# Attention and soft-MoE on one core: larger input loads, far masks on VectorE, and single-bank PSUM tiles in the tail

## The chip, the core and the metric

The kernel runs on one core of one Trainium2 chip. The metric is device time in microseconds (us). A core has TensorE (PE, matmuls, its weight loads shown apart as PEld), VectorE (DVE), ScalarE (ACT), GpSimd (POOL), SyncE (SP) and 16 DMA engines. All operands of matmuls lie in SBUF; results go to PSUM[...].

## The reference, cut to what matters

```python
# q, k, v: (4 batches, 8 heads, 768 positions, 64), all float32
scores = (q @ k.transpose(0, 1, 3, 2)) / 8.0
causal = rel >= 0                                   # rel = row position - column position
stream_keep = causal & (is_sink | (rel < 64))       # is_sink: the first 4 columns
mask = where(is_retrieval[head], causal, stream_keep)
a = softmax(where(mask, scores, -1e9))              # over the columns
x = (a @ v).transpose(0, 2, 1, 3).reshape(3072, 512)

logits = x @ phi                                    # phi: (512, 32); 8 experts, 4 slots each
d = softmax(logits, axis=0)                         # over the tokens
slot_input = (d.T @ x).reshape(8, 4, 512)
slot_out[e] = relu(slot_input[e] @ w1[e]) @ w2[e]   # w1: (512, 1024), w2: (1024, 512) per expert
out = softmax(logits, axis=1) @ slot_out            # (3072, 512) float32
```

Three of the eight heads are "retrieval" heads (full causal mask), the others keep a window of 64 and the first four columns. Which head is which is an input that is read on the chip.

## The kernel before

The order of all work is written out by hand (a manual schedule): each engine runs its instructions in the order in which the program names them, and the framework adds the semaphore waits. The work has three stages.

**Attention** goes over 16 pairs of heads, `n` from 0 to 15 (pairs 0 to 3 are batch 0, and so on). `load_qk` (L104) and `load_v` (L111) bring the pair's q, k and v from memory; DMAs issued on POOL turn float32 into bf16 on the way. `transposes` (L135) turns q or k on PE, `evac` (L143) copies the result out of PSUM, q on DVE, k on ACT. `scores` (L159) makes one of six chunks of the transposed scores and their exponentials on ACT (L171); `mask` (L173) multiplies chunks by the mask on DVE; `vfar` (L153) multiplies the far blocks of v by `fmask`; `pvmm` (L185) multiplies by v, `norm` (L195) divides by the row sums. The loop at L318 is pipelined: iteration `n` makes the scores of pair `n`, the PV products of pair `n-1`, and the transposes of q and k of pair `n+1`; q's come after the second chunk of scores in PE's order, k's after the fourth.

The loads run ahead. Iteration `n` issues k, q and v of pair `n+3` (L319 to L322), and one or two half weight matrices (`w_load`, L119: 26 halves of `w1` and of the first five `w2`). The raw tiles of q and k have three buffers, v has five tiles (`vbs`, L100). Two things hold an issue back on POOL: a buffer still in use, and the framework's eight DMA semaphores: a DMA waits for the eighth one before it. All these DMAs go through one queue.

`fmask` (per head and far block, whether a key counts) is filled at the start by ACT, two copies for each of eight heads (L301 to L303).

**Routing** is woven into the loop: per batch, `x_transpose`, `logits_mm`, `logits_exp`, `exp_tokens` and `dispatch_mm` make the logits, their exponentials and the unnormalized slot inputs; `slot_sum` adds the latter over the batches. The last batch does this after the loop (L398 to L419). There all six token blocks go to one PSUM tile, which ACT and DVE copy by halves (L254, L255).

**The tail.** The last three `w2` matrices have no place of their own: `w2_5` takes the masks' place, `w2_6` and `w2_7` that of the probabilities, so their loads (L389 to L408) wait for the end of the loop. From L427 on: slot inputs (`sip`, `siT`), first layer into the two-bank tiles `hp` (L439), ReLU by ACT on one half and DVE on the other (L443, L444), transposes of the hidden layer (L450), row sums for the output (`rp`, L462), and the second layer (`second`, L467), where four experts stand side by side on 32 output partitions each. `sp` is copied to `slot_out` by halves (L476, L477). Then 24 blocks of 128 output rows (L479 to L492): a matmul into half of a two-bank tile `op`, even rows read by DVE, odd rows by ACT, and a DMA on SP after 1, 1, 2 and then each 4 rows.

Of the kernel before, what the change touches and what calls it, by code (L numbers as in the profile page):

```python
# [10 lines left out]
F32 = mybir.dt.float32  # L11
BF16 = mybir.dt.bfloat16
I32 = mybir.dt.int32
ALU = mybir.AluOpType
ACT = mybir.ActivationFunctionType
# [3 lines left out]
NP = 16  # L19
# [19 lines left out]
def kernel(  # L39
# [13 lines left out]
    nc = tc.nc  # L53
    P = 128
    B, H, S, D = q.shape
    n_sink, window = int(n_sink), int(window)
    ES = moe_phi.shape[1]
    NE, DM, F = moe_w1.shape
    SPE = ES // NE
    scale = 1.0 / (D ** 0.5)  # L60
    ent = ctx.enter_context
# [3 lines left out]
    raw = ent(tc.tile_pool(name="raw", bufs=3))  # L65
    qkT = ent(tc.tile_pool(name="qkT", bufs=2))
# [3 lines left out]
    xp = ent(tc.tile_pool(name="xp", bufs=2))  # L70
    scp = ent(tc.tile_pool(name="scp", bufs=2, space=PSUM))
# [3 lines left out]
    def single(shape, dt, name, tag=None):  # L75
        return singles.tile(shape, dt, name=name, tag=tag or name)
# [3 lines left out]
    ident = single([P, P], BF16, "ident")  # L80
# [7 lines left out]
    slot_bf = single([P, 2, DM], BF16, "slot_bf")  # L88
# [11 lines left out]
    vbs = [single([P, 2, 6, 66], BF16, f"vb{i}") for i in range(5)]  # L100
# [3 lines left out]
    def load_qk(n, which):  # L104
        b, h = n // 4, 2 * (n % 4)
        src, d = (q, qraw) if which == "q" else (k, kraw)
        t = raw.tile([P, 2, 384], BF16, tag="r" + which, name="r" + which)
        nc.gpsimd.dma_start(t, src[b, h:h + 2].rearrange("h (p s) d -> p h (s d)", s=6))  # L108
        d[n] = t

    def load_v(n):  # L111
        b, h = n // 4, 2 * (n % 4)
        a = v[b, h:h + 2]
        nc.gpsimd.dma_start(vbs[n % 5].rearrange("p h j d -> p (h j) d")[:, :, :D],  # L114
                            a.rearrange("h (j p) d -> p (h j) d", p=P))
# [3 lines left out]
    def w_load(count):  # L119
        for _ in range(count):  # L120
            i = wi[0]
            wi[0] += 1
            if i >= 4 * NE - 6:
                return
            e, half = (i % (2 * NE)) // 2, i % 2
            if i < 2 * NE:
                nc.gpsimd.dma_start(  # L127
                    w1s[e][:, 2 * half:2 * half + 2, :],
                    moe_w1[e].rearrange("(di do) f -> di do f", do=4)[:, 2 * half:2 * half + 2, :])
            else:  # L130
                nc.gpsimd.dma_start(
                    w2s[e][:, 4 * half:4 * half + 4, :],
                    moe_w2[e].rearrange("(fi fo) d -> fi fo d", fo=8)[:, 4 * half:4 * half + 4, :])
# [19 lines left out]
    def vfar(n):  # L153
        h = 2 * (n % 4)
        t = vfp.tile([P, 2, 4, 66], BF16, tag="vf", name="vf")
        nc.vector.tensor_mul(t, vbs[n % 5][:, :, :4, :], fmask[:, h:h + 2])
        vf[n] = t
# [27 lines left out]
    def pvmm(n, i):  # L185
        if i % 3 == 0:
            pv[n] = pvp.tile([P, 3, 2, 65], F32, tag="pv", name="pv")
        for hh in range(2):
            for j in range(i + 1):
                vv = vbs[n % 5] if i - j <= 1 else vf[n]  # L190
                o = BLK[j, i]
                nc.tensor.matmul(pv[n][:, i % 3, hh, :], pT[n][:, hh, o:o + 128], vv[:, hh, j, :D + 1],  # L192
                                 start=(j == 0), stop=(j == i))
# [43 lines left out]
    def dispatch_mm(b, i0=0, i1=6):  # L237
        if i0 == 0:
            sps[b] = pvp.tile([P, DM], F32, tag="pv", name="slp")
        for i in range(i0, i1):  # L240
            g = i % 4
            nc.tensor.matmul(sps[b][32 * g:32 * g + 32, :], elgs[b][:, i, :], xb[b][:, i, :],
                             start=(i < 4), stop=(i + 4 >= 6))

    def slot_sum(b):
        sp = sps[b]
        if b == 0:
            nc.vector.tensor_copy(slot_acc, sp)
        elif b == B - 2:
            nc.vector.tensor_add(slot_bf[:, 0], slot_acc, sp)  # L250
        elif b < B - 1:
            nc.vector.tensor_add(slot_acc, slot_acc, sp)
        else:
            nc.scalar.copy(slot_bf[:, 1, :256], sp[:, :256])  # L254
            nc.vector.tensor_copy(slot_bf[:, 1, 256:], sp[:, 256:])  # L255


    load_qk(0, "k")
    load_qk(0, "q")
# [6 lines left out]
    load_qk(1, "k")  # L266
    load_qk(1, "q")
    load_v(1)
    w_load(1)
    load_qk(2, "k")  # L270
    load_qk(2, "q")
    load_v(2)
# [27 lines left out]
    V.memset(vbs[0][:, :, :, D:], 1.0)  # L300
    for h in range(H):  # L301
        nc.scalar.copy(fmask[:, h], r1[:, h:h + 1].rearrange("p (o d) -> p o d", o=1).to_broadcast([P, 4, 66]))
        nc.scalar.copy(fmask[:, h, 0], r0[:, h:h + 1].to_broadcast([P, 66]))  # L303
    for t in vbs[1:]:
        V.memset(t[:, :, :, D:], 1.0)

# [11 lines left out]
    for n in range(NP):  # L318
        if n + 3 < NP:  # L319
            load_qk(n + 3, "k")  # L320
            load_qk(n + 3, "q")
            load_v(n + 3)  # L322
        w_load(2 if n % 3 == 2 else 1)
# [54 lines left out]
        if n < 3:  # L378
            for h in (2 * n + 2, 2 * n + 3):
                head_mask(h)  # L380
        elif n == 3:
            setup_late()


    w_load(4 * NE)
# [3 lines left out]
    def w2_late(e):  # L389
        for half in range(2):  # L390
            nc.gpsimd.dma_start(w2s[e][:, 4 * half:4 * half + 4], w2v[e][:, 4 * half:4 * half + 4])  # L391

    w2_late(5)
    w2s[6] = ptp.tile([P, 8, DM], BF16, tag="pT", name="w2_6")
    w2_late(6)
# [12 lines left out]
    w2_late(7)  # L408
# [10 lines left out]
    slot_sum(bl)  # L419
# [7 lines left out]
    sip = trp.tile([P, 4, ES], F32, tag="tr", name="sip")  # L427
    sv = [slot_bf[:, x].rearrange("p (di do) -> p do di", do=4) for x in range(2)]
    for do in range(4):
        for x in range(2):  # L430
            nc.tensor.matmul(sip[:, do], sv[x][:, do], sum4, start=(x == 0), stop=(x == 1))
    V.tensor_copy(siT, sip)
    hs = []
    for e4 in range(2):
        hp = scp.tile([P, 2, 512], F32, tag="sc", name="hp")
        for c in range(2):
            for do in range(4):
                for g in range(4):
                    nc.tensor.matmul(hp[32 * g:32 * g + 32, c], siT[:, do],  # L439
                                     w1s[4 * e4 + g][:, do, c * 512:(c + 1) * 512],  # L440
                                     start=(do == 0), stop=(do == 3))
        t = xp.tile([P, 2, 512], BF16, tag="xb", name="hs")
        nc.scalar.activation(t[:, 0], hp[:, 0], ACT.Relu, scale=emask[:, e4:e4 + 1])  # L443
        V.tensor_scalar(t[:, 1], hp[:, 1], emask[:, e4:e4 + 1], 0.0, op0=ALU.mult, op1=ALU.max)  # L444
        hs.append(t.rearrange("p c f -> p (c f)").rearrange("p (fi fo) -> p fo fi", fo=8))
    hT = []
    for e4 in range(2):
        tp = trp.tile([P, 8, P], BF16, tag="tr", name="tph")
        for fo in range(8):
            nc.tensor.transpose(tp[:, fo, :], hs[e4][:, fo, :], ident)  # L450
        t = qkT.tile([P, 8, P], BF16, tag="hT", name="hT")
        if e4 == 0:
            V.tensor_copy(t, tp)
        else:
            nc.scalar.copy(t, tp)
        hT.append(t)
    rp = trp.tile([P, 24], F32, tag="tr", name="rp")
# [6 lines left out]

    sp = pvp.tile([P, DM], F32, tag="pv", name="sp")

    def second(e4, gs):  # L467
        for fo in range(8):
            for g in gs:
                nc.tensor.matmul(sp[32 * g:32 * g + 32, :], hT[e4][:, fo, 32 * g:32 * g + 32],  # L470
                                 w2s[4 * e4 + g][:, fo, :],
                                 start=(e4 == 0 and fo == 0), stop=(e4 == 1 and fo == 7))

    for e4, gs in ((0, (0, 1, 2, 3)), (1, (0, 1)), (1, (2,)), (1, (3,))):
        second(e4, gs)
    V.tensor_copy(slot_out[:, :256], sp[:, :256])  # L476
    nc.scalar.copy(slot_out[:, 256:], sp[:, 256:])  # L477
# [3 lines left out]
    for t, rows in enumerate((1, 1, 2, 4, 4, 4, 4, 4)):  # L481
        ot = single([P, rows, DM], F32, f"ot{t}", tag=f"w1_{t}")
        for y in range(0, rows, 2):
            op = scp.tile([P, 2, DM], F32, tag="sc", name="op")
            for x in range(min(2, rows)):
                nc.tensor.matmul(op[:, x], er[r], slot_out, start=True, stop=True)  # L486
                if r % 2:
                    nc.scalar.activation(ot[:, y + x], op[:, x], ACT.Copy, scale=rrow[:, r:r + 1])  # L488
                else:
                    V.tensor_scalar(ot[:, y + x], op[:, x], rrow[:, r:r + 1], None, op0=ALU.mult)  # L490
                r += 1
        nc.sync.dma_start(ov[:, r - rows:r, :], ot)  # L492
# [35 lines left out]
```

The softmax here doesn't subtract the row's maximum and nothing guards it: scores larger than these inputs give would overflow.

## Time and profile before

| | us |
|---|---|
| median of 6 runs (lowest, highest) | 170.03 (169.53, 170.54) |
| the profiled execution | 169.53 |
| its span on the core | 167.7 |
| busy PE, PEld | 121.1, 71.7 |
| busy DVE, ACT, POOL | 102.0, 113.6, 58.5 |

Busy times are unions of an engine's instructions, of a span of 167.7 us. POOL's busy time is nearly all the making of DMA descriptors (0.7 us for a q or k, 1.02 for a v, 0.56 for half a weight). The memory traffic is 52.50 MB read and 6.29 MB written. In the page, a line such as "L171 ACT" names line 171 of the kernel; the 40 digits of a row are tenths of busy time in 40 equal slices of the span. In the chain of waits each row has a start, a duration and an instruction, and the row above is what it waited for. In the timeline, a bracket tells how long the engine had been idle and what ended that.

### The profile page before, as it was taken

The numbers are of one execution on the slowest core, as the hardware profiler recorded it, in microseconds if no ns is written. First come the engines' busy times: TensorE is split into PE (matmuls) and PEld (weight loads), VectorE is DVE, ScalarE is ACT, GpSimd is POOL, SyncE is SP. The second block draws the span as 40 slices with busy tenths as digits, with TensorE's granted clock in tenths as the row PEclk, the third lists the DMA queues.
The fourth block names the chain that finished last, engine by engine and source line by source line (L and its number), as shares of the span: only waits on it lengthen the run. The fifth ranks groups of instructions, "written<-read, shape, count | busy, mean of one in ns | idle before, by whom it ended". The sixth has DMA issues, their size and how long they took to land. (4 is left out here: it accounts for less than half of the span.)

```text
span 167.7 us, 4099 instructions
## 1 busy us (share of the span) xinstructions
PE 121.1 (72%) x1752; PEld 71.7 (43%) x1752; DVE 102.0 (61%) x226; ACT 113.6 (68%) x162; POOL 58.5 (35%) x89
## 2 busy tenths in 40 slices
PE   0455987977969977969979787988597965555430
PEld 0332555654546555636556555556235621111100
DVE  2846489999839879836898756887305004334410
ACT  3699899999888999977999978892312102334330
POOL 7994555563554454462542615006100000000000
PEclk9999999999999999996999996999969996555555
DMA  3999999999999999999999999999999941566665
GB/s 48 145 180 190 201 193 194 192 212 191 204 198 193 210 193 195 201 200 204 198 192 196 210 193 211 212 213 217 211 214 212 216 86 44 206 250 250 250 279 221
DMA packets 39985, 32.80 MB, mean 196 GB/s; under 512 B 26656, under 2 KB 34848, under 8 KB 39328
## 3 DMA queue, kind: packets, MB, share of 16 engines
q0 software_dynamic: 38672, 26.25, 105.3%
q1 hardware_dynamic: 1296, 6.30, 9.2%
q8 instruction: 13, 0.21, 0.5%
q14 instruction: 4, 0.03, 0.0%
HBM read 52.50 MB, written 6.29 MB: 351 GB/s over the span
## 5 line engine op out<-in xcount | busy, mean ns | idle before, releaser
L171 ACT ACTIVATE pT<-sc 128x1024 bf16<-128x1024 f32 (+1 forms) x96 | 83.5, 928 | 8.4 <-PE sc L166 7.6
L166 PE MATMUL sc<-Tq,Tk 64*128 64x256 bf16 (+3 forms) x320 | 37.4, 301 | 16.7 <-ACT Tk L150 9.0
L192 PEld LDWEIGHTS <-pT 128*128 128x128 bf16 x672 | 25.0, 99 | 11.3 <-issue 8.3
L183 DVE TENSOR_TENSOR pT<-pT,msk 128x1024 bf16<-128x1024 bf16 (+1 forms) x48 | 29.3, 640 | 0.1
L192 PE MATMUL pv<-vb,pT 128*128 128x65 bf16 x352 | 27.5, 197 | 0.0
L192 PE MATMUL pv<-vf,pT 128*128 128x65 bf16 x320 | 25.2, 197 | 0.0
L114 POOL DMA_DIRECT2D vb<-in_v_dram x16 | 16.5, 1032 | 22.2 <-DVE pT L183 5.2
L166 PEld LDWEIGHTS <-Tk 64*128 64x128 bf16 x320 | 12.2, 96 | 27.4 <-ACT Tk L150 11.8
L486 PE MATMUL op<-slot_out,expT 128*128 128x512 bf16 x24 | 12.3, 606 | 10.6 <-DVE ot L490 9.7
L201 DVE TENSOR_TENSOR xb<-pv,rs 128x384 bf16<-128x384 f32 x32 | 17.8, 557 | 1.1
L147 DVE COPY Tq<-tpq 128x768 bf16<-128x768 bf16 x16 | 15.3, 957 | 4.9 <-PE tpq L140 4.9
L488 ACT ACTIVATE ot<-op,rrow 128x512 f32<-128x512 f32 x12 | 8.2, 687 | 14.5 <-PE op L486 14.5
L200 DVE RECIPROCAL rs<-pv 128x6 f32<-128x6 f32 x32 | 6.2, 194 | 18.3 <-PE pv L192 18.2
L490 DVE TENSOR_SCALAR ot<-op,rrow 128x512 f32<-128x512 f32 x12 | 9.0, 751 | 12.8 <-PE op L486 12.8
L150 ACT COPY Tk<-tpk 128x768 bf16<-128x768 bf16 x16 | 13.0, 814 | 3.6 <-PE tpk L140 3.6
L108 POOL DMA_DIRECT2D rk<-in_k_dram x16 | 11.5, 718 | 7.2 <-PE sc L166 3.2
L140 PE MATMUL tpk<-ident,rk 128*64 128x128 bf16 x192 | 9.1, 234 | 5.3 <-DMA rk<-in_k_dram 4.7
L108 POOL DMA_DIRECT2D rq<-in_q_dram x16 | 11.5, 716 | 2.8 <-DMA vb<-in_v_dram 2.6
L127 POOL DMA_DIRECT2D w<-in_moe_w_dram x16 | 9.0, 565 | 8.3 <-DMA w<-in_moe_w_dram 7.4
L140 PE MATMUL tpq<-ident,rq 128*64 128x128 bf16 x192 | 10.0, 251 | 2.4 <-DMA rq<-in_q_dram 2.4
L486 PEld LDWEIGHTS <-expT 128*128 128x128 bf16 x24 | 3.8, 157 | 17.7 <-issue 17.7
L140 PEld LDWEIGHTS <-rk 128*64 128x64 bf16 x192 | 6.5, 116 | 8.9 <-DMA rk<-in_k_dram 4.7
(70 smaller groups left out, 118.2 us busy)
## 6 DMA issues: line engine op xcount, KB each, us to landing
w<-in_moe_w_dram POOLq DMA_DIRECT2D x32, 512.0 KB, 12.3
out_dram<-ot SPq DMA_DIRECT2D x5, 1024.0 KB, 3.8
rk<-in_k_dram POOLq DMA_DIRECT2D x16, 192.0 KB, 11.3
rq<-in_q_dram POOLq DMA_DIRECT2D x16, 192.0 KB, 11.5
vb<-in_v_dram POOLq DMA_DIRECT2D x16, 192.0 KB, 10.8
out_dram<-ot SPq DMA_DIRECT2D x2, 256.0 KB, 2.2
out_dram<-ot SPq DMA_DIRECT2D x1, 512.0 KB, 2.6
phi<-in_moe_phi_dram POOLq DMA_DIRECT2D x1, 32.0 KB, 11.1
```

Source lines behind the costliest of these rows:

```text
L108: nc.gpsimd.dma_start(t, src[b, h:h + 2].rearrange("h (p s) d -> p h (s d)", s=6))
L114: nc.gpsimd.dma_start(vbs[n % 5].rearrange("p h j d -> p (h j) d")[:, :, :D], a.rearrange("h (j p) d -> p (h j) d", p=P))
L127: nc.gpsimd.dma_start(w1s[e][:, 2 * half:2 * half + 2, :], moe_w1[e].rearrange("(di do) f -> di do f", do=4)[:, 2 * half:2 * half + 2, :])
L140: nc.tensor.transpose(tp[64 * hh:64 * hh + 64, s, :], src[:, hh, 64 * s:64 * s + 64], ident)
L147: nc.vector.tensor_copy(o, i)
L150: nc.scalar.copy(o, i)
L166: nc.tensor.matmul(sc[:, hh, at:at + 128 * cnt], kT[n][po:po + 64, j * 128:(j + 1) * 128], qT[n][po:po + 64, i0 * 128:(i0 + cnt) * 128], s ...
L171: nc.scalar.activation(pT[n][:, :, o:o + ln], sc[:, :, :ln], ACT.Exp, scale=scale)
L183: nc.vector.tensor_mul(x, x, m)
L192: nc.tensor.matmul(pv[n][:, i % 3, hh, :], pT[n][:, hh, o:o + 128], vv[:, hh, j, :D + 1], start=(j == 0), stop=(j == i))
L201: nc.vector.tensor_mul(xb[b][:, 3 * half:3 * half + 3, h * D:(h + 2) * D].rearrange("p i (h d) -> p i h d", h=2), pv[n][:, :, :, :64], rs. ...
L486: nc.tensor.matmul(op[:, x], er[r], slot_out, start=True, stop=True)
```

## The change

- q and k are loaded for four heads (two pairs) in one DMA, from pair 2 on; pairs 0 and 1 keep loads of two heads. v is loaded for four heads from the start. In odd iterations `n`, the loads of pairs `n+3` and `n+4` are issued. Raw tiles have two buffers of twice the size, v has three tiles of twice the size.
- A weight matrix is one DMA, and the pace is written as a total: `w_load(upto)`. Only `w2_7` keeps two halves.
- The far masks are made by DVE, two copies for two heads at a time: the first pair's at the start, the others' in iterations 0 to 2.
- In the last batch the six token blocks go to two PSUM tiles of three blocks each; both are copied by DVE, and `sip` sums three terms instead of two.
- From `sip` on, PSUM tiles are one bank for one reader (`bank`): `hp` per half, the transposes of the hidden layer four at a time with one copy each on DVE and ACT, `sp` as two tiles of 256 columns (so `second` has twice the matmuls, each of 256 columns), and `op` one row per tile, from six tiles in turn.
- The order of the tail on PE changes: transposes of the first four experts, their second layer, transposes of the others, second layer of experts 4 and 5, `rp`, then experts 6 and 7.

```diff
-    raw = ent(tc.tile_pool(name="raw", bufs=3))
+    raw = ent(tc.tile_pool(name="raw", bufs=2))
...
-    vbs = [single([P, 2, 6, 66], BF16, f"vb{i}") for i in range(5)]
+    vbs = [single([P, 4, 6, 66], BF16, f"vb{i}") for i in range(3)]
...
+    def load_qk(pairs, which):
+        b, h, c = pairs[0] // 4, 2 * (pairs[0] % 4), 2 * len(pairs)
...
+        t = raw.tile([P, c, 384], BF16, tag="r" + which, name="r" + which)
+        nc.gpsimd.dma_start(t, src[b, h:h + c].rearrange("h (p s) d -> p h (s d)", s=6))
+        for x, n in enumerate(pairs):
+            d[n] = t[:, 2 * x:2 * x + 2]
...
+    def w_load(upto):
+        while wi[0] < min(upto, 2 * NE - 3):
+            e = wi[0] % NE
+            if wi[0] < NE:
+                nc.gpsimd.dma_start(w1s[e], moe_w1[e].rearrange("(di do) f -> di do f", do=4))
+            else:
+                nc.gpsimd.dma_start(w2s[e], moe_w2[e].rearrange("(fi fo) d -> fi fo d", fo=8))
+            wi[0] += 1
...
+    load_qk([0], "k")
+    load_qk([0], "q")
...
     load_v(0)
-    load_qk(1, "k")
-    load_qk(1, "q")
-    load_v(1)
-    w_load(1)
-    load_qk(2, "k")
-    load_qk(2, "q")
-    load_v(2)
+    load_qk([1], "k")
+    load_qk([1], "q")
     w_load(1)
...
-    for h in range(H):
-        nc.scalar.copy(fmask[:, h], r1[:, h:h + 1].rearrange("p (o d) -> p o d", o=1).to_broadcast([P, 4, 66]))
-        nc.scalar.copy(fmask[:, h, 0], r0[:, h:h + 1].to_broadcast([P, 66]))
-    for t in vbs[1:]:
+    def far_mask(n):
+        h = 2 * n
+        V.tensor_copy(fmask[:, h:h + 2, 1:], r1[:, h:h + 2].rearrange("p (h a d) -> p h a d", a=1, d=1).to_broadcast([P, 2, 3, 66]))
+        V.tensor_copy(fmask[:, h:h + 2, 0], r0[:, h:h + 2].rearrange("p (h d) -> p h d", d=1).to_broadcast([P, 2, 66]))
+
+    for t in vbs:
         V.memset(t[:, :, :, D:], 1.0)
+    far_mask(0)
+    load_qk([2, 3], "k")
+    load_qk([2, 3], "q")
+    load_v(1)
+    w_load(2)
...
     for n in range(NP):
-        if n + 3 < NP:
-            load_qk(n + 3, "k")
-            load_qk(n + 3, "q")
-            load_v(n + 3)
-        w_load(2 if n % 3 == 2 else 1)
+        if n % 2 == 1 and n + 4 < NP:
+            for which in ("k", "q"):
+                load_qk([n + 3, n + 4], which)
+            load_v((n + 3) // 2)
+        w_load(2 + (5 * (n + 1) + 1) // 7)
...
         if n < 3:
+            far_mask(n + 1)
             for h in (2 * n + 2, 2 * n + 3):
                 head_mask(h)
...
-    slot_sum(bl)
+    V.tensor_copy(slot_bf[1][:96], sps[bl, 0][:96])
+    V.tensor_copy(slot_bf[2][:96], sps[bl, 3][:96])
...
+    def bank(t, shape=(P, 512), dt=F32):
+        pool, tag = ((scp, "sc"), (trp, "tr"), (pvp, "pv"))[t]
+        return pool.tile(list(shape), dt, tag=tag, name="bank")
...
-        hp = scp.tile([P, 2, 512], F32, tag="sc", name="hp")
+        t = xp.tile([P, 2, 512], BF16, tag="xb", name="hs")
         for c in range(2):
+            hp = bank(0 if e4 == 0 else 2)
...
+    def turn(e4):
+        t = qkT.tile([P, 8, P], BF16, tag="T" + "qk"[e4], name="hT")
+        for x in range(2):
+            tp = bank(1, (P, 4, P), BF16)
+            for fo in range(4):
+                nc.tensor.transpose(tp[:, fo, :], hs[e4][:, 4 * x + fo, :], ident)
+            if x:
+                nc.scalar.copy(t[:, 4:], tp)
+            else:
+                V.tensor_copy(t[:, :4], tp)
+        hT[e4] = t
+
+    sp = [bank(0, (P, 256)) for x in range(2)]
+
+    def second(e4, gs):
+        for fo in range(8):
+            for x in range(2):
+                for g in gs:
+                    nc.tensor.matmul(sp[x][32 * g:32 * g + 32, :], hT[e4][:, fo, 32 * g:32 * g + 32],
+                                     w2s[4 * e4 + g][:, fo, 256 * x:256 * x + 256],
+                                     start=(e4 == 0 and fo == 0), stop=(e4 == 1 and fo == 7))
+
+    turn(0)
+    second(0, (0, 1, 2, 3))
+    turn(1)
+    second(1, (0, 1))
+    rp = bank(1, (P, 24))
...
+    second(1, (2,))
+    second(1, (3,))
+    V.tensor_copy(slot_out[:, :256], sp[0])
+    nc.scalar.copy(slot_out[:, 256:], sp[1])
...
-        for y in range(0, rows, 2):
-            op = scp.tile([P, 2, DM], F32, tag="sc", name="op")
-            for x in range(min(2, rows)):
-                nc.tensor.matmul(op[:, x], er[r], slot_out, start=True, stop=True)
...
+        for y in range(rows):
+            op = bank((1, 2, 0)[r % 3])
+            nc.tensor.matmul(op, er[r], slot_out, start=True, stop=True)
+            if r % 2:
+                nc.scalar.activation(ot[:, y], op, ACT.Copy, scale=rrow[:, r:r + 1])
+            else:
+                V.tensor_scalar(ot[:, y], op, rrow[:, r:r + 1], None, op0=ALU.mult)
+            r += 1
```

## The prediction

> **What bounds the kernel now.** I read the slices of the page first, then the chain of waits, then the DMA issues, then the timelines of GpSimd (POOL) and TensorE (PE).
>
> ```profile
> DMA  3999999999999999999999999999999941566665
> GB/s 48 145 180 190 201 193 194 192 212 191 204 198 193 210 193 195 201 200 204 198 192 196 210 193 211 212 213 217 211 214 212 216 86 44 206 250 250 250 279 221
> ```
>
> A slice is 4.19 us. The DMA engines are full from slice 1 to slice 31 (134 us): the kernel reads 52.5 MB in one stream. After it they are half busy.
>
> ```profile
> 118.42 19.38 DMA w<-in_moe_w_dram
> 137.79 0.04 issue
> 137.84 1.04 PE sp L470 x4
> 138.87 0.02 issue
> 138.90 0.43 DVE slot_out L476
> 139.33 0.02 issue
> 139.35 0.38 ACT slot_out L477
> ...
> 144.48 1.02 PE op L486 x2
> 145.51 0.03 issue
> 145.53 0.76 DVE ot L490
> 146.29 0.04 issue
> ```
>
> The chain: the last weight lands at 137.8, `sp` is done at 138.87, and then 28.8 us of output follow. There a pair of rows takes 1.85 us, since matmuls and both readers take turns on one two-bank `op` tile. Before 137.8 there is slack: PE waited 1.43 us for that weight (L470), so `sp` could have ended at 138.87 - 1.6 = 137.27.
>
> In the attention loop ScalarE (ACT) sets the pace: 5.7 us a pair, some 8 in pairs 5, 9, 13. What can break this pace is the arrival of q and k. Two answers about pair 14's q, the issue and the time to landing, and PE's use of it:
>
> ```profile
> 81.80 0.71 POOL L108 DMA_DIRECT2D rq<-in_q_dram  x1
> ```
> ```profile
> DMA to landing us min/median/max: 12.0/12.0/12.0
> ```
> ```profile
> 94.72 0.53 PE L140 MATMUL tpq<-ident,rq 128*64 128x128 bf16 x12
> ```
>
> It lands at 93.8 and is transposed at 94.7: under 1 us to spare. Landings follow the order of issue. In a full queue a k or q of two heads adds 0.99 us, a v 1.27, half a weight 2.45 (the last six land at 125.5, 128.0, 130.5, 132.9, 135.3, 137.8).
>
> **What the Trainium skill says.** "DMA: Bandwidth & Descriptors", section Bandwidth: larger DMAs are better, 341 GB/s at 1 MB, 425 at 16 MB, and 435 is the ceiling. Here half a weight is 1.05 MB of f32 in 2.45 us, 428 GB/s: queued behind others it is already there, so size can bring 1.6% of the weights' time. "PSUM — Partial Sum Buffer", section PSUM bank collisions: two engines may not use one bank at once. The trace agrees: ACT's `slot_out` starts 0.02 us after VectorE's (DVE) has ended. "TensorE: Matmul & The Clock Gate", section LDWEIGHTS: time goes with the columns, by its formula an estimated 27 ns for 32; the trace has 43 ns (L439, 0.17 for four). Same page, Part 1: an idle PE drops to half clock; granted here was 0.50 from 140 us on.
>
> **The change, part by part.**
>
> *Loads of four heads, whole weights.* The same bytes and rows in fewer DMAs (44 instead of 81 from POOL). The order matters: loads for two pairs come at once, and k of both, q of both stand in front of what is used first. Weights now run ahead: in front of pair 14's q stand ten whole weights, where eight (16 halves) stood before. Sum to that landing: pair 1's q at 10.5 + 1.3 (one v more in front) = 11.8; 7 k and 7 q at 1.98 = 27.7; 6 v at 2.54 = 15.2; 10 weights at 4.90 = 49.0; phi 0.3: 104.0. The same sum for pair 15's q before gives 10.5 + 28 x 0.99 + 14 x 1.27 + 18 x 2.45 + 0.3 = 100.4, where the trace has 102.2, so 1.7% is missing: 105.7. Fewer DMAs may save something: in the trace the 4-byte completion packets took 1.63 us of all 16 engines for 81 DMAs, 0.02 each, 0.6 for the 30 fewer up to there; with the 1.6% of 49 us at most 1.4. Bounds 104.0 and 106; I take 105.2. PE wants it at 94.7. The same sum for the others: pair 2 at 20.7 (wanted 18.7), 4 at 32.9, 6 at 49.3, 8 at 60.4, 10 at 76.7, 12 at 88.2; with the delay carried along, stalls of some 2, 0.5, 4, 0, 2, 0, and at 14 the rest. PE may fall to half clock after such stalls, which costs the next pair up to 1 us (pair 14 took 7.2 at half clock, pair 12 took 5.7); as pair 14's q comes at a time of its own, only the last such loss counts, and the loop of before had one there too (102 to 106). The queue never runs dry on the way: a load of pairs n+3, n+4 waits for the raw tile of pairs n-1, n, free one iteration earlier, with over 7 us of stream in front. Behind that wait on POOL stand q, v and the weights of the same step; they would land later than the queue ahead in any case. The phi copies on POOL (L328) now wait for phi's landing near 28, and k of pairs 6 and 7 stands behind them; it waits for its raw tile until 31 anyway. POOL's own time per DMA (0.7 for a k, 1.02 for a v, 0.56 for a weight) at most doubles for four heads and stays under a third of the DMA's. The `v` tiles are three for two pairs each; the oldest was last read by a PV product two iterations before it is loaded again, so that wait is over. So the loop shifts by 105.2 - 94.7 - 0.3 = 10.2 us (0.3 is what PE runs ahead of ACT): behind the waiting transposes on PE stand the scores of the third chunk, behind them ACT's exponentials and DVE's masks, all in order. After pair 14 nothing more is loaded for the loop, so its last part takes what it took, 114.1 - 94.7. The loop ends at 114.1 + 10.2 = 124.3.
>
> The late weights wait for the loop: `w2_5` for the masks (issued at 113.2, now 123.4), when the stream (23.1 MB, landed at 123.0 as before) is just dry: 2 us lost, last landing near 140. That is before PE comes.
>
> *Far masks.* 16 ACT copies go (6.3 to 11.3 us, 0.41 and 0.25 each). The first exponential comes 1.8 us earlier, but the third needs pair 1's q, 11.8: no gain. DVE gets two copies a pair; not shown before, between the 0.25 + 0.41 of ACT's and nothing, 0.6 taken. The wait for pair 2 hides them; without it DVE, 94% busy from 20 to 30 us, would pass on up to 4 x 0.6.
>
> *Tail up to `sp`.* Two full-width DVE copies at 0.7 (0.42 for 256 columns) for a 0.37 and a 0.42 in turn, one of them early: +0.3. hp in single banks: `hs` starts after its own bank, so the first transposes' copies end near 128.6 instead of 129.5, and `second(0)` starts there instead of at 131.2. But `second` now has 128 matmuls of 256 columns, four groups side by side 0.108 us a step, with four weight loads of 43 ns a step: 16 steps at 0.11 to 0.17, 1.7 to 2.75; I take 2.2. Then transposes and copies of the second half stand bare: 1.4. Then 1.73, the 24 `rp` matmuls 1.75 (they lay under a copy before), and 3.0 for the two single groups. From 128.9: 2.2 + 1.4 + 1.75 + 1.75 + 3.0 + 0.3 = 10.4, 139.3 against 137.27: +2.0 (bounds +1.3, +2.6; 1.7 less if the half clock of 122.7 to 126.1 isn't granted again).
>
> *Output.* Both `slot_out` copies at once: 0.45 instead of 0.86. Six single-bank tiles let PE, DVE and ACT run free (a matmul waits for the reader of six rows before, long done): 24 matmuls at 0.43 = 10.3 us, DVE 12 x 0.79 = 9.5. The DMA's own time is longer: 9.2% of the span, 15.4 us (408 GB/s). From the end of `sp`: 0.45 + 0.64 + 0.80 = 1.9 to the first row; 0.85 to its first packet; 15.4 and 0.3 of gaps; 0.35 to the last landing; 1.35 to the end (166.34 to 167.7): 20.2 instead of 28.8. A sustained write at 370 GB/s would add 1.6.
>
> **Sum.** `sp` ends at 137.27 + 10.2 + 2.0 = 149.5; + 20.2 = 169.7. The span was 167.7, its execution took 169.53, the median of the runs is 170.03. +2.0 gives 172.0. Break-even: 8.6 of output, plus 1.6 of slack, less 2.0 of tail: a shift of 8.2 us.
>
> **The rivals.** (1) On the other side: the loads come earlier than my sum, and the shift stays under 8.2. That needs pair 14's q before 103.2, so weights at 4.7 or the 1.7% not paid, or a tail without the half clock. For it: fewer, larger DMAs; against it: 428 GB/s is reached already. With a shift of 7 and a tail of +1: 167.8. (2) The loads aren't late at all, weights being taken out of order or beside: then the last weight (137.8) or the tail (139.3) sets `sp`: 139.3 + 20.2 = 159.5, 161.8 as a median. Against it: every landing of before is in order. (3) The edit of PSUM does not bring what it says: a write at 370 GB/s and weight loads at full price, +1.6 and +0.6: 174.2; if reads kept taking turns as before, 8 us more.
>
> **Chances.** Forecast 0.62 (own range 169.8 to 174), rival 1 0.22, rival 2 0.07, rival 3 0.09. 167.0 to 174.5 leaves out rival 2 and the outer part of 3 and 1, under 0.2. A change of 0.3% (0.5 us) is about what a measurement of this kernel can tell from none. Slower: most of the forecast and rival 3, 0.66; within: 0.07; faster: rivals 1 and 2, 0.27.
>
> **What would show it.** PE waiting for rq in pairs 1, 5, 9, 13, the last one ending near 105; the last exponential ending near 124; no wait of PE for the last weight; DMA 0.9 busy in the output, 20 us from the end of `sp`. Wrong if pair 14's q lands before 103, or the output takes over 22 us.

## The result, and the profile after

The changed kernel takes 169.92 us in the median of 35 runs (167.89 to 174.31); the kernel before, in 72 runs, 169.53 (167.67 to 171.46, and one of 204.54). The medians differ by 0.4 us, and the ratio is 1.0001, with a 95% interval of 0.998 to 1.0022: no change that can be measured, where a slowdown of 2 us had been forecast as the likeliest. Ratios and intervals, here and below, are taken over the runs within 1.5% of a kernel's fastest, which leaves out nearly half of the changed kernel's. The profiled execution of the changed kernel took 171.84 us with a span of 170.1, 2 us more than the median, so times are read from it with that in mind. The median span of the runs is 168.1.

First the slices of the page after (one slice is 4.25 us):

```profile
PEclk9999999999978999999879997596999879999955
DMA  3999999999999999999999999999129995009995
GB/s 51 133 217 198 181 226 183 195 215 218 186 191 205 189 213 216 195 186 219 192 191 220 210 192 190 216 216 208 35 29 191 216 205 107 4 2 408 422 420 227
```

Two things changed in the DMA row. The stream of loads has a gap at slices 28 and 29 (119 to 128 us): the last weights wait for the end of the loop, which is later. And the output, from slice 36, moves 408 to 422 GB/s, where before it never passed 279. In the clock row the output begins at full clock, where before it had half. The clock row of before:

```profile
PEclk9999999999999999996999996999969996555555
```

Now the chain of waits of the changed kernel, from the end of the loop on:

```profile
121.47 3.57 ACT pT L167 x4
...
134.34 5.35 PE bank L437 x64
...
140.85 1.93 PE bank L466 x64
142.78 0.41 PE bank L453 x4
143.19 0.02 issue
143.21 0.43 DVE hT L457
143.65 0.04 issue
143.69 1.92 PE bank L466 x32
145.62 1.75 PE bank L479 x24
147.37 3.19 PE bank L466 x32
...
151.43 3.88 DVE ot L496 x6
```

No weight is in it: before, the row ahead of `sp` was a DMA. Now the chain comes from the exponentials of the last pair (L167) and never leaves the engines, and in the output DVE's rows follow each other without PE between them.

Last the loop. The issue of pair 14's q on POOL, its time to landing, and its use on PE:

```profile
89.03 0.77 POOL L108 DMA_DIRECT2D rq<-in_q_dram  x1
```

```profile
DMA to landing us min/median/max: 15.2/15.2/15.2
```

```profile
104.24 0.85 PE L136 MATMUL tpq<-ident,rq 128*64 128x128 bf16 x12 [1.39 <-DMA rq<-in_q_dram]
```

89.03 + 15.2 = 104.2, and PE, idle for 1.39 us before it, starts at once. Before the change it started at 94.72 and did not wait. Only this last 1.39 us of the delay of 9.5 us was waited at pair 14, though: PE had waited 2.94 us for pair 1's q (1.27 before), 1.99 for pair 2's and 2.42 for pair 6's (none and 0.33 before), and had had 3.4 us at half clock from 49.3 and from 83.4 us on. The other landings lie as forecast (in brackets): pair 2 at 21.0 (20.7), 4 at 32.6 (32.9), 6 at 48.9 (49.3), 8 at 60.2 (60.4), 10 at 76.3 (76.7), 12 at 87.5 (88.2), 14 at 104.2 (105.2).

### The profile page after: what moved, and what is told of

It reads as the page before. It is cut to its first block, busy times and chain, and to the rows that moved or that the text cites. A ratio compares the mean times of both kernels' runs of the same rounds, so it can differ in the third digit from the quotient of the medians.

```text
span 170.1 us, 4185 instructions
## 1 busy us (share of the span) xinstructions
PE 122.1 (72%) x1820; PEld 77.8 (46%) x1820; DVE 104.2 (61%) x234; ACT 108.6 (64%) x146; POOL 36.7 (22%) x52
## 5 line engine op out<-in xcount | busy, mean ns | idle before, releaser
L167 ACT ACTIVATE pT<-sc 128x1024 bf16<-128x1024 f32 (+1 forms) x96 | 84.0, 926 | 24.7 <-PE sc L162 23.9
L162 PE MATMUL sc<-Tq,Tk 64*128 64x256 bf16 (+3 forms) x320 | 38.4, 307 | 14.9 <-ACT Tk L146 8.2
L188 PE MATMUL pv<-vb,pT 128*128 128x65 bf16 x352 | 28.5, 201 | 0.0
L143 DVE COPY Tq<-tpq 128x768 bf16<-128x768 bf16 x16 | 15.3, 956 | 12.3 <-PE tpq L136 12.2
L108 POOL DMA_DIRECT2D rk<-in_k_dram x9 | 6.8, 755 | 47.6 <-PE tpk L136 46.8
L136 PEld LDWEIGHTS <-rq 128*64 128x64 bf16 x192 | 7.3, 130 | 14.1 <-DMA rq<-in_q_dram 11.6
L114 POOL DMA_DIRECT2D vb<-in_v_dram x8 | 11.7, 1467 | 1.3 <-DMA w<-in_moe_w_dram 0.5
L206 DVE COPY xT<-tpx 128x768 bf16<-128x768 bf16 (+1 forms) x17 | 9.0, 530 | 1.4 <-PE tpx L205 1.3
L205 PE MATMUL tpx<-ident,xb 128*128 128x128 bf16 x96 | 9.1, 233 | 0.5 <-DVE xb L197 0.3
L496 DVE TENSOR_SCALAR ot<-bank,rrow 128x512 f32<-128x512 f32 x12 | 8.0, 745 | 0.5 <-PE bank L492 0.5
L215 PE MATMUL lg<-xT,phi 128*128 128x384 bf16 x32 | 7.5, 378 | 0.9 <-ACT expT L219 0.5
L494 ACT ACTIVATE ot<-bank,rrow 128x512 f32<-128x512 f32 x12 | 7.3, 696 | 0.9 <-PE bank L492 0.7
## 6 DMA issues: line engine op xcount, KB each, us to landing
rq<-in_q_dram POOLq DMA_DIRECT2D x7, 384.0 KB, 15.2
```

The lines of the kernel that those rows point to most:

```text
L114: nc.gpsimd.dma_start(vbs[m % 3].rearrange("p h j d -> p (h j) d")[:, :, :D], v[b, h:h + 4].rearrange("h (j p) d -> p (h j) d", p=P))
L136: nc.tensor.transpose(tp[64 * hh:64 * hh + 64, s, :], src[:, hh, 64 * s:64 * s + 64], ident)
L143: nc.vector.tensor_copy(o, i)
L162: nc.tensor.matmul(sc[:, hh, at:at + 128 * cnt], kT[n][po:po + 64, j * 128:(j + 1) * 128], qT[n][po:po + 64, i0 * 128:(i0 + cnt) * 128], s ...
L167: nc.scalar.activation(pT[n][:, :, o:o + ln], sc[:, :, :ln], ACT.Exp, scale=scale)
L205: nc.tensor.transpose(tp[:, i * 128:(i + 1) * 128], xb[b][:, i, hp * 128:(hp + 1) * 128], ident)
```

## The experiments

**Theory A**: the forecast's mechanism. Weights ahead of q in the one queue bring pair 14's q late, the loop and everything behind it shifts, and the single-bank output gives nearly the same amount back; the size of the shift beyond the landing depends on what clock TensorE is granted in the last pairs. **Rival B**: the cost of the loads lies in their form (four heads, whole matrices) or in another part of the edit, such as the far masks, and not in what stands ahead of pair 14's q; then the order of the weights matters little.

The runs in one table (us; read from the traces, by the end of the last exponential, of `sp`, and of the span):

| kernel | loop end | `sp` end | span | loop to `sp` | `sp` to end | median of runs |
|---|---|---|---|---|---|---|
| before | 114.1 | 138.9 | 167.7 | 24.7 | 28.8 | 169.5 |
| after | 126.4 | 150.6 | 170.1 | 24.1 | 19.5 | 169.9 |
| e1 after again | 122.9 | 147.0 | 166.5 | 24.1 | 19.5 | 169.8 |
| e2 tail alone | 114.4 | 139.3 | 158.8 | 24.9 | 19.6 | 160.6 |
| e3 loads alone | 125.4 | 148.9 | 177.2 | 23.6 | 28.2 | 179.4 |
| e4 far masks alone | 115.2 | 139.4 | 168.2 | 24.2 | 28.8 | 169.6 |
| e5 weights later | 118.3 | 143.1 | 162.6 | 24.8 | 19.5 | 164.6 |
| e6 weights later still | 115.7 | 139.8 | 159.4 | 24.1 | 19.6 | 160.6 |
| e7 output pairs as before | 124.9 | 148.6 | 176.1 | 23.7 | 27.5 | 177.2 |
| e8 warm | 123.9 | 149.1 | 168.7 | 25.3 | 19.6 | 169.8 |
| e9 one weight more | 130.1 | 154.0 | 173.6 | 24.0 | 19.6 | 175.4 |
| e10 e6, rows earlier | 116.8 | 139.0 | 158.6 | 22.2 | 19.5 | 159.8 |
| e11 e10, one weight less | 113.4 | 138.6 | 158.1 | 25.2 | 19.6 | 159.1 |

A span is 1.7 to 1.9 us shorter than the time of its execution.

### e1: the changed kernel again

No edit.

> The changed kernel once more, for a second profile. Theory A (the sum of the prediction, with terms mended): pair 14's q lands near 104.2 whatever the clock does, the output takes 19.5 us from the end of the second layer, and only the clock windows between the transposes of pair 14 and the end of the loop differ: an execution near the median (169.9) has one half-clock window of 3.4 us there, the profiled one had three, so the loop ends near 124 instead of 126.4. Theory B (the stream of loads varies from run to run): pair 14's q lands 1 to 2 us earlier or later than 104.2. Both: 169.9.

Measured: 169.84 us in the median of 22 runs, ratio to before 1.0024 (1.0 to 1.0049); the profiled execution is 3.6 us shorter than the first one, 166.5 of span. The landing of pair 14's q is the same, 104.4, and PE uses it at once:

```profile
104.41 0.53 PE L136 MATMUL tpq<-ident,rq 128*64 128x128 bf16 x12 [0.39 <-DMA rq<-in_q_dram]
```

The two part after it. The stretch from this transpose to the last exponential, in both (columns: stretch, its length, busy PE, PEld, DVE, ACT, POOL with counts, granted clock, DMA share, GB/s), first of the changed kernel, then of e1, then of the kernel before:

```profile
104.24:126.43 22.19, 19.54 (x267) 12.12 (x267) 13.81 (x29) 15.94 (x22) 0.58 (x2) 0.78 0.77 148
```

```profile
104.41:122.86 18.45, 15.63 (x267) 10.11 (x267) 13.82 (x30) 16.56 (x23) 0.59 (x2) 1.00 0.90 177
```

```profile
94.72:114.11 19.39, 16.73 (x269) 10.74 (x267) 14.38 (x30) 16.97 (x24) 4.19 (x9) 0.91 1.18 209
```

The same 267 matmuls take 15.6, 16.7 or 19.5 us of PE, by a clock of 1.00, 0.91 or 0.78, and the stretch grows by as much. So the same program with the same landings ends its loop at 122.9 or 126.4: the loop's shift has two terms, the landing, and the clock after it. That says nothing yet about B. Nor is the landing itself fixed, as theory B of this run had it: with the same loads the same q landed at 104.9 in e3 and e8 and at 106.1 in e7.

### e2: the tail alone

The changed tail, with the loads and far masks of before. The core of the edit, against the changed kernel:

```diff
-        w_load(2 + (5 * (n + 1) + 1) // 7)
+        if n + 3 < NP:
+            load_qk(n + 3, "k")
+            load_qk(n + 3, "q")
+            load_v(n + 3)
+        w_load(2 if n % 3 == 2 else 1)
```

> The loads, buffers and far masks of before, with the tail of after from the last batch's slot inputs on. Theory A (parts add up: the tail and the output are on the path by themselves): the loop ends at 114, the second layer ends near 138.5 (the last weight at 137.8 sets it), 19.5 us of output: span 158, time 160.0, ratio 0.943. Theory B (neither part moves the time, since the kernel is bound by its memory traffic as a whole): 169.5.

Measured: 160.55 us, ratio 0.9517 (0.9455 to 0.9579). Its chain of waits:

```profile
118.74 19.44 DMA w<-in_moe_w_dram
138.18 0.04 issue
138.22 1.05 PE bank L471 x8
```

The last weight sets `sp` again, as before, so the tail's own length is hidden and the output's whole saving arrives: 28.8 - 19.6 = 9.2 us of the span, less 0.4 for a later `sp`. This also shows what the changed kernel would have taken had the loads cost nothing.

### e3: the loads alone

The changed loads, with far masks and tail of before:

```diff
-    far_mask(0)
+    for h in range(H):
+        nc.scalar.copy(fmask[:, h], r1[:, h:h + 1].rearrange("p (o d) -> p o d", o=1).to_broadcast([P, 4, 66]))
+        nc.scalar.copy(fmask[:, h, 0], r0[:, h:h + 1].to_broadcast([P, 66]))
...
-            op = bank((1, 2, 0)[r % 3])
+            op = scp.tile([P, 2, DM], F32, tag="sc", name="op")
```

> The loads of after (four heads, whole weights, their pace), with the tail and the far masks of before. Theory A: pair 14's q lands at 104.2, the loop ends between 124 and 126.5, 23.2 us of tail as before without the wait for the last weight, 28.8 of output: span 176 to 178.5, time 178 to 180, ratio 1.05 to 1.06. Theory B (neither part moves the time): 169.5.

Measured: 179.37 us, ratio 1.0609 (1.0551 to 1.0666). In the chain of waits `sp` (L462) now follows the engines' own work, and the output still takes turns:

```profile
143.62 5.33 PE sp L462 x64
...
157.68 1.02 PE op L478 x2
```

The two halves of the change are both large: -9.0 us (e2) and +9.9 us (e3) against 169.5. Their sum is +0.9, uncertain by some 1.4 us (either interval is 1 us to each side); the whole change shows +0.4. No third effect is needed: two real effects cancel.

e3 also shows how long the old second layer takes when all its weights are there: 64 matmuls from 143.55 to 148.94, 5.39 us. Before, the same 64 took from 131.21 to 138.86:

```profile
131.21 5.20 PE L470 MATMUL sp<-w,hT 128*32 128x512 bf16 x60
137.84 1.02 PE L470 MATMUL sp<-w,hT 128*32 128x512 bf16 x4 [1.43 <-DMA w<-in_moe_w_dram]
```

That is 7.65 us, so the late weights cost 2.26 us there, and not the 1.6 of the forecast. The bracket of 1.43 us shows the last wait alone. The first half of the same matrix landed at 135.34, and its first matmul started at 135.38; that wait lies beside work of the group before it and leaves no gap. Without both waits the old tail would take 131.21 + 5.39 - 114.11 = 22.5 us from the end of the loop to `sp`. e3's own 23.6 says the same: its first layer had a lower clock and took 6.36 us, where 5.32 were taken before.

### e4: the far masks alone

The kernel before, with the far masks made by DVE:

```diff
-    for h in range(H):
-        nc.scalar.copy(fmask[:, h], r1[:, h:h + 1].rearrange("p (o d) -> p o d", o=1).to_broadcast([P, 4, 66]))
-        nc.scalar.copy(fmask[:, h, 0], r0[:, h:h + 1].to_broadcast([P, 66]))
+    far_mask(0)
...
         if n < 3:
+            far_mask(n + 1)
```

> Before with the far masks alone made by VectorE, two heads at a time. Theory A: nothing on the path, the third exponential waits for pair 1's q: within 0.3% of before, 169.5. Rival: VectorE, over 90% busy from 20 to 40 us, passes its 4 x 0.6 us on to the loop: the loop ends up to 1.5 us later; the slack of 1.6 us before the last weight hides that, so the end of the loop in the profile tells it, not the time.

Measured: 169.64 us, ratio 1.0011 (0.9984 to 1.0037). The first exponential comes 2.4 us earlier (8.78 instead of 11.16), but the lead shrinks from pair to pair and is 0.3 us by the first exponential of pair 5; pair 6 then waits 1.17 us for its q. DVE's copies for a pair take 1.2 us at the start and 0.6 to 0.9 in the loop, where the forecast took 0.6. Whether they are what takes the lead back is not shown: DVE is full from 30 to 40 us in this run (first line; columns as in e1, DVE is the third busy time), but it was so before (second line).

```profile
30.00:40.00 10.00, 8.04 (x152) 5.43 (x150) 9.74 (x28) 9.13 (x12) 5.77 (x10) 1.00 1.29 199
```

```profile
30.00:40.00 10.00, 8.63 (x166) 5.69 (x163) 9.74 (x28) 9.66 (x12) 5.09 (x7) 1.00 1.30 201
```

The loop ends 1.1 us later than before, which was the rival's sign; but pair 14's q is taken up at 94.59, 0.13 us earlier than before, and after it this execution had 6.8 us at half clock, where before had 3.4. The far masks neither gain nor lose; they aren't B's hidden cost.

### e5 and e6: weights later in the queue

The same DMAs of the same size; only when a weight is issued changes. In e5 (the first edit) eight whole weights stand ahead of pair 14's q instead of ten; in e6 (the second) eight as well, none ahead of pairs 2 and 3, and one less ahead of pairs 4 and 6.

```diff
-        w_load(2 + (5 * (n + 1) + 1) // 7)
+        w_load((2, 2, 3, 3, 4, 4, 5, 6, 7, 7, 8, 9, 10, 11, 12, 13)[n])
```

```diff
-    w_load(1)
...
-    w_load(2)
+    w_load(1)
...
-        w_load(2 + (5 * (n + 1) + 1) // 7)
+        w_load((1, 2, 2, 3, 4, 5, 5, 6, 6, 7, 8, 9, 10, 11, 12, 13)[n])
```

> The changed kernel with its weights held back in the loop: eight whole weights in front of pair 14's q instead of ten (three instead of four in front of pair 6's), everything else as in after. Theory A (weights that overtake q and k delay the loop): pair 14's q lands 9.7 us earlier, near 94.7; only the wait for pair 2's q stays (2 us); the loop ends near 116, the second layer near 140, span 159.5, time 161.3, ratio 0.952. Rival (the loads of four heads delay the loop by their size, whatever the weights do): pair 14's q is late by the same 9 us, 169.9.

> As the run with the weights held back, and besides no weight in front of pairs 2 and 3, one less in front of 4 and 6. Theory A: no wait for q over 0.5 us in the loop; it ends near 114, the stream of loads ends near 136.5, the second layer near 138, 19.5 us of output: span 157.5, time 159.3, ratio 0.940; some 2 us less than the run before it. Rival (once the loop is on time, the last weight alone sets the end): the same as the tail alone with the loads of before, 160.5.

Measured: e5 164.6 us (161.7 to 166.24, four runs, too spread for an interval); e6 160.59 us, ratio 0.9461 (0.9412 to 0.951). In e5 pair 14's q lands at 94.4 and PE takes it up at 98.92 without a wait, 4.2 us later than before. Of this 2.6 us are there at pair 2, after waits for the q of pair 1 (3.13 us) and of pair 2 (1.99); the rest arises between pairs 2 and 6, and its cause is not traced. The expectation had counted 2 us, so the loop ends 2.3 us later than expected. In e6 nothing waits for pair 2's q (pair 1's is still waited for, 3.01 us), and its loop ends at 115.7. The form of the loads is that of the changed kernel in both, so B's "form" is refuted: the cost is the weights' place in the queue. e6 takes 1.3 us more than theory A said. That it meets the rival's 160.5 is chance: its last weight lands at 136.2, and `sp` ends 3.6 us later, after 24.1 us of the tail's own work.

### e7: output by pairs as before

```diff
-            op = bank((1, 2, 0)[r % 3])
-            nc.tensor.matmul(op, er[r], slot_out, start=True, stop=True)
+            op = scp.tile([P, 2, DM], F32, tag="sc", name="op")
+            for x in range(min(2, rows)):
+                nc.tensor.matmul(op[:, x], er[r], slot_out, start=True, stop=True)
...
```

> The changed kernel with the output rows in two-bank tiles for two rows again, as before; everything else as in after. Theory A (the output is on the path by itself): 1.85 us for two rows again, 28.4 us from the end of the second layer instead of 19.5: plus 8.9, time 178.8, ratio 1.055. Rival (the output DMAs set the time anyway): plus 1 at most, 170.9.

Measured: 177.16 us, ratio 1.0457 (1.0416 to 1.0499); 7.3 us over the changed kernel, where 8.9 were expected. From `sp` to the end 27.5 us. The chain of waits shows the turns, 1.85 us for two rows:

```profile
154.80 1.02 PE op L493 x2
...
155.85 0.76 DVE ot L497
...
156.65 1.02 PE op L493 x2
```

So 8.0 of the output's 9.3 us come from this one edit. Of the 1.3 left over, 0.45 is `slot_out` by both engines at once (from `sp` to the first matmul 0.46 us here, 0.91 before). The other 0.8 is the clock: the first turns take 1.2 us here and in e3, where neither tail nor output was changed, and 1.4 before.

### e8: PE kept busy through the waits

Ten matmuls more, of the identity with 512 columns of mask, whose result nobody reads, ahead of the waiting transposes in iterations 5, 9 and 13:

```diff
+            if n in (5, 9, 13):
+                fill = trp.tile([P, 512], F32, tag="tr", name="fill")
+                for _ in range(10):
+                    nc.tensor.matmul(fill, ident, msk[:, 0, :512], start=True, stop=True)
             tq = transposes(n + 1, "q")
```

> The changed kernel with ten matmuls of 512 columns, whose results nobody reads, ahead of the transposes of q in iterations 5, 9 and 13, where TensorE waits for q: they add 2.2 us of work to waits of 1 to 3 us and change no output. Theory A (the spread between executions, 166 to 172 us of span, comes from half-clock windows after those waits): fewer such windows, median near 168.3 instead of 169.9 and less spread. Rival (the windows follow from the iterations with the logits, not from the waits): nothing gained, or up to 2 us lost where the filling comes late.

Measured: 169.75 us, ratio 1.0009 (0.9976 to 1.0043), runs from 168.04 to 173.16. The clock row of the page shows no reduced clock before slice 31 (131 us), where the changed kernel had four stretches:

```profile
PEclk9999999999999999999999999999999569999965
```

From pair 14's transposes to the last exponential this execution takes 18.45 us, as e1 did. But the median gains nothing, and the 14 runs spread as widely as the 22 of e1 (168.28 to 172.46), against theory A. The filler itself delays the transposes (pair 14's start at 105.4, where they could have started at 104.9), and the half clock now comes in the tail, for 6.8 us instead of 3.4: from the end of the loop to `sp` it is 25.3 us instead of 24.1. Of the 58 executions of the changed kernel on record, the half with the lower granted clock took 170.6 us in the median, the other half 169.6. So the clock accounts for a part of the spread; that warming pays is not shown.

Nor does the run tell waits for q from the rival, since the filler stands in the very iterations with the logits. The traces do. The clock changes at the edges of a grid of 3.41 us, which lies differently in each execution. Between 20 and 112 us, the 13 traces have 28 stretches of this grid at full clock that were followed by half clock; PE was busy in 0.18 to 0.59 of each. 288 were followed by full clock, and in all but three of them PE was busy in more than 0.59; in e8 none was under 0.60. (Earlier, at 18 to 19 us, seven stretches of 0.39 to 0.42 were followed by full clock; why is open.) Some of them:

| trace | stretch (us) | PE busy (us) | clock of the next |
|---|---|---|---|
| after | 100.46 to 103.87 | 1.55 | 0.50 |
| after | 110.70 to 114.11 | 1.84 | 0.50 |
| e1 | 103.51 to 106.92 | 3.02 | 1.00 |
| e1 | 110.34 to 113.75 | 2.52 | 1.00 |
| before | 98.80 to 102.22 | 1.85 | 0.50 |

The first holds the wait for pair 14's q. In the last PE waited for no q: ACT, busy for 3.38 of the 3.42 us, set the pace. So, as far as these traces go, both theories have a part: waits for q bring the half clock, and so do the iterations where PE waits for ACT, whenever enough of the idle time falls into one stretch. PE need not be idle for it, as the forecast had put it: being busy for half of a stretch was too little.

### e9: one weight more

```diff
-        w_load(2 + (5 * (n + 1) + 1) // 7)
+        w_load(2 + (5 * (n + 1) + 1) // 7 + (n == 10))
```

> The changed kernel with one more whole weight in front of pair 14's q (eleven instead of ten, issued in iteration 10), nothing else. Theory A: that q lands 4.85 us later, near 109.2, and the end of the loop and the time follow in full: 169.8 plus 4.85 is 174.6, ratio about 1.03. Rival (there is slack behind the loop's last wait, in the clock or in the late weights): 171 or less.

Measured: 175.4 us, ratio 1.0402 (1.0345 to 1.0459). Pair 14's q on PE:

```profile
110.07 0.85 PE L136 MATMUL tpq<-ident,rq 128*64 128x128 bf16 x12 [4.59 <-DMA rq<-in_q_dram]
```

It comes 5.7 us later than in e1: 0.3 us of this is there at pair 12 already, and from that landing to pair 14's the queue takes 5.3 us longer. The median is 5.6 us longer: one to one. From ten weights on there is no slack left.

### e10 and e11: a better version

e6 with the tail's row sums (`rp`) moved ahead of `sip`, and k and q of pair 1 ahead of the first v (e10); then seven weights ahead of pair 14's q (e11). The edit of e10 against e6, and that of e11 against e10:

```diff
-    load_v(0)
     load_qk([1], "k")
     load_qk([1], "q")
+    load_v(0)
...
+    rp = bank(1, (P, 24))
+    er = []
+    for r in range(24):
+        e = expT.rearrange("c b t -> c (b t)").rearrange("c (p r) -> c r p", r=24)[:, r]
+        er.append(e)
+        nc.tensor.matmul(rp[:, r:r + 1], e, quarter, start=True, stop=True)
+    V.reciprocal(rrow, rp)
     sip = bank(1, (P, 4, ES))
...
```

```diff
-        w_load((1, 2, 2, 3, 4, 5, 5, 6, 6, 7, 8, 9, 10, 11, 12, 13)[n])
+        w_load((1, 2, 2, 3, 4, 5, 5, 6, 6, 7, 7, 9, 10, 11, 12, 13)[n])
```

> The run with the weights held back further (160.6), with k and q of pair 1 loaded ahead of the first v, and the row sums of the output (24 matmuls) moved from between the second layers to ahead of the slot inputs, where TensorE waits for VectorE. Theory A: the third exponential comes 2 us earlier and so does the loop's end, near 113.5; the move of the 24 matmuls gives 0.8; the second layer is then set by the last weight (136.2 plus 1.05), 137.3: span 156.8, time 158.5. Rival (the loop's early gain is given back by VectorE, as with the far masks alone): 159.8.

> The run before it with one weight less in front of pair 14's q (seven instead of eight), nothing else. In that run TensorE waited for this q (it landed at 94.6, wanted at 92.5) and half-clock windows followed. Theory A: that q lands near 89.8, nothing waits; the loop ends near 113.5, the second layer at 137.4, set by the last weight; span 157, time 158.7. Rival (the wait was not what cost; the half-clock windows come with the iterations of the logits): 159.8 again.

Measured: e10 159.76 us, ratio 0.944 (0.9398 to 0.9482); e11 159.05 us, ratio 0.9402 (0.9359 to 0.9444). e10's loop was faster up to pair 13 and so ran into pair 14's q again:

```profile
94.66 0.85 PE L136 MATMUL tpq<-ident,rq 128*64 128x128 bf16 x12 [2.14 <-DMA rq<-in_q_dram]
```

From there to its last exponential it took 22.15 us at a clock of 0.79. So e10 stays 1.3 us above theory A, and that it meets the rival's 159.8 is chance: what was gained early (4.8 us against e6 at pair 13) was lost at this wait and in the half clock after it, not to VectorE. In e11 that wait is gone, its loop ends 3.4 us earlier (113.4), and the chain of waits ends where that of the kernel before ended, at the last weight:

```profile
116.02 21.47 DMA w<-in_moe_w_dram
137.49 0.04 issue
137.54 1.05 PE bank L472 x8
```

So `sp` comes only 0.4 us earlier than in e10, and the times of the two do not differ beyond their intervals. e11 is 6% faster than both kernels; what bounds it is the stream of loads, as at the start, and then an output that the DMA engines fill.

## Why the prediction was wrong

The mechanism held in the main: PE waits for q, adding or removing weights ahead of q moves the time (e9, e6), the last weight is no longer waited for, the DMA engines are 0.9 busy in the output. Two of the rows by which the forecast wanted to be judged did not come. In iteration 9 PE did not wait, since it was late itself and came for pair 10's q at 76.32, when that had landed at 76.3; and the last exponential ended at 126.4 and 122.9 in the two traces, not near 124. In e7 PE, late from the waits before, did not wait at pair 14 either. But what made the answer wrong is the balance. The forecast is a small difference of terms near 10 us each; several costs were set too dear, and together they were as large as the answer. By the forecast's own steps:

- **Loads, landing of pair 14's q: 105.2 forecast, 104.2 to 104.4 measured.** The plain sum, 104.0, was nearly right. The correction of 1.7%, taken from one landing of the kernel before, was not paid: a whole weight mostly took 4.85 us, not 4.90. From pair 4 to pair 12 the landings lay 0.2 to 0.7 under the sum; then one weight ahead of pair 14's q took 5.6 us (6.2 in e1) and gave that back. The rival on the other side had named just this ("the 1.7% not paid"), though its own test, a landing before 103.2, was not met.
- **"Its last part takes what it took": 19.4 forecast, 18.45 to 22.2 measured.** It was taken as a constant. The windows of e1 show that it is 18.45 at full clock and 22.2 at 0.78. In e1 the loop ends at 122.9, under the forecast's 124.3; in the profiled execution of the changed kernel at 126.4, over it. From the median span (168.1, less 24.1 and 19.5) it follows as 124.5: inferred, though e7 and e3, with the same loads, ended it at 124.9 and 125.4. That this is close to the forecast is luck: the landing was put 1 us too late and the part after it about 1 us too short.
- **The step that failed: the sum of "Tail up to `sp`", 25.2 us from the end of the loop (139.3 - 114.1) forecast, 24.1 measured.** By the chain above: `second(0)` starts 14.4 us after the loop, where 14.8 were taken with 0.3 for the slot copies, and these cost nothing, as from the last dispatch matmuls to the end of `siT` it is 2.05 us in e1 and 2.06 before. `second(0)` itself took 1.93 where 2.2 was taken, so the four weight loads of a step did not set the pace; transposes and copies of the second half 0.9 (0.41 + 0.02 + 0.43 + 0.04) where 1.4 was taken, since the four transposes of one half lie beside the copy of the other. `rp` (1.75) came as forecast, the last two groups took 3.2, where 3.0 and the 0.3 that ends that sum were taken, and the pair of groups before them 1.92 instead of 1.75, the one term that was too cheap. The half clock during `hp`, on which 1.7 us more would have hung, was granted again (at 130.8 in e1).
- **The slack before the last weight: 1.6 forecast, 2.26 measured** (see e3). The forecast's "+2.0" set the new tail against an `sp` at 137.27; by that yardstick it came as +0.95, below both bounds. But without its waits the old tail would have ended at 136.6, so that the change lengthened the tail by 1.6 us (24.1 against 22.5), within the bounds, and had more slack to do it in. The misreading moves 0.7 us from one term to another and leaves their sum alone.
- **Output: 20.2 forecast, 19.5 measured.** The first matmul took 0.41 us at full clock where 0.64 had been taken from a PE at half clock, and the first issue to the last landing took 16.5 instead of 16.9.
- **Far masks: no change forecast, none measured** (e4).
- **The late weights:** the forecast had the last landing near 140 and saw it hidden. It was 143.1 in the longer execution and hidden.
- **From span to median:** +2.3 forecast, from the six runs shown; 1.8 measured, as six runs had put the median of before 0.5 us too high.

At the median this makes 1.1 of tail and 0.7 of output, less 0.2 of loop: the 1.6 us by which the change came out smaller, +0.4 instead of +2.0. With 0.5 of base it is the 2.1 us from 172.0 to 169.9. The break-even point, put at a shift of 8.2 us, was 9.3 of output, plus 2.26 of slack, less 1.64 of tail: 9.9. The shift was 8.75 in e1, 12.3 in the profiled execution and, by the inference above, 10.4 at the median. The change sits on its own break-even point. That the profiled span of 170.1 nearly equals the forecast's 169.7 is no support for it: there a loop 2.1 us too long hides a tail and an output 1.8 us too short.

Not settled are where the rest of the loop's delay in e5 arises, and why the same queue brings pair 14's q at 104.2 in one execution and at 106.1 in another (e7, where pair 1's q was 1.5 us late already).

## What to carry to other kernels

When a change is the sum of a gain and a loss of like size, forecast the break-even point and its uncertainty before the sign; here a tenth of either term decides. A load merged with its neighbours should be costed by what now stands ahead of it in its queue, and what merging brings can be kept while the order is mended: issue late what is needed late, which turned a ratio of 1.00 into 0.94. Where a profile shows a stretch at a reduced clock, ask for the same stretch at full clock before it is carried over as a constant. And take the slack ahead of a wait from a run that does not wait: the bracket of a wait shows only its last part.

## What the runs showed of the hardware

Two executions of one program, with equal landings, differed by 3.6 us of span through stretches of half clock. In the loop, with few exceptions, half clock followed stretches of 3.41 us in which PE was busy for less than 0.59, whether it waited for a DMA or for ACT; the grid of these stretches lay differently in each execution. The output ran at 408 to 422 GB/s in the middle slices; no run shows the 370 that the forecast feared. And 64 matmuls of 256 columns in four groups side by side took 1.93 us, 0.12 a step of four; their 64 weight loads kept PEld busy for 1.65 us of it, 26 ns each, where the forecast had taken 43 from another line. The loads lay beside the matmuls and did not set the pace.
